# A fused attention, expert and feed-forward kernel: another order of copies, casts and sums in its last stage

## The chip, the cores and the metric

The kernel runs on one core of a Trainium2 chip. The metric is the device time of one execution in microseconds (us), the median of several runs. The engines are called as in the profile: PE is TensorE (matmuls; PEld its weight loads), ACT ScalarE, DVE VectorE, POOL GpSimd, SP the engine that issues most DMAs. SBUF is the on-chip memory, PSUM the memory that matmuls write to.

## What is computed

Three parts run one after the other: an attention over pooled keys, a layer of eight experts, and a feed-forward layer. The change lies in the last, which takes 4608 tokens of 512 values through 2048 hidden values:

```python
def _moe2_ref(x, w_in, w_out):          # x 4608x512, w_in 512x2048, w_out 2048x512
    h = x @ w_in
    g = h * (1.0 / (1.0 + np.exp(-h)))  # silu
    return (g @ w_out).astype(np.float32)
```

## The kernel before

**Numbers as pairs.** Every float32 operand of a matmul is a pair: a high part (a cast on ACT to the type fp32r) and a low part (the rest, a subtraction on DVE or POOL). A product is three matmuls into one PSUM tile: high by high, high by low, low by high. So nothing goes to PE before ACT has cast it and, two matmuls later, DVE has made its low part.

**Visits.** Tokens are taken in nine blocks of 512. The first three go through the feed-forward layer directly, in four visits (the loop over `visits` in `ffn`, line 1599; the first block in two visits, of 6 and 10 steps, the others in 16 each). One step `f` handles 128 hidden values: `mm1` (12 matmuls into a tile fh; then silu on ACT into fsg, a cast into fgh, a subtraction on DVE into fgl) and `mm2` of the step before (12 matmuls into fop), so 24 matmuls of 128x512 a step. Beside this, visits 0 and 1 build the pairs of the layer's weights (DVE, ACT, POOL) and write them to DRAM, and during the last two visits a generator `sums()` (line 1314) forms sums of the weights for what follows. One of its 16 steps adds high and low parts on DVE (two instructions into a tile sw), forms four sums on POOL, casts them on ACT and subtracts on DVE (into a tile shl), and writes the pair with two DMAs. In the kernel before, a step begins with the cast and subtraction of the sums made just before it; the tile sw has one buffer (tag fr0).

**Double blocks.** The other six token blocks are taken two by two, each pair as a 2x2 block matrix, by the seven-product scheme of Strassen and Winograd, in both matmuls of the layer. There are 12 rounds `m` (line 1657): three double blocks, with four rounds of 512 hidden values each. A round has three runs of matmuls on PE:

- `strassen(2m)`, here *even*: seven products of 6 matmuls (tiles ps), from the token sums (xc) and the weight sums (win),
- `strassen(2m+1)`, here *odd*: the same with the next weights (w1l),
- `second(m)`: seven parts of 12 matmuls (tiles fopy), 6 with the even and then 6 with the odd combination c_k of the hidden values, and the weights wout.

Between them, ACT, DVE and POOL turn products into hidden values (copies tm, silu into hs), add these into the combinations (`sum1` to `sum4`, into cs and in place) and make the pair c_0 to c_6 of each (`combo`: the cast on ACT; it returns the subtraction on DVE, called the low part; `split2`: both at once). `evict` adds a finished part of `second` into an accumulator accc, on ACT as a copy where a double block begins. Four parts of `second` add onto the PSUM tile of two parts before, so such a part begins after that eviction.

**What sets the order.** Each engine executes in the order in which the code records instructions: there is no scheduler behind it. The code is written as a sequence with hooks: `strassen` calls `hook(i)` after its i-th product and `second` calls `hook(e)` after half parts, and the work of the run before is recorded there. So an instruction that waits holds back all behind it on its engine; SP's DMAs likewise.

## Time and profile before

| what | value |
|---|---|
| median of 3 runs | 1355.88 us (1355.69 to 1356.69) |
| the profiled execution: its own time | 1355.27 us |
| its span in the trace | 1353.3 us |
| PE busy | 1238.0 us, 91% of the span |
| DVE busy | 932.7 us, 69% |
| ACT busy | 612.7 us, 45% |
| POOL busy | 390.5 us, 29% |
| mean share of the 16 DMA engines (queue q1) | 56.6% |
| mean granted PE clock | 0.967 of full |

The span runs from the first to the last instruction in the trace. Matmuls overlap, so PE counts as busy a little longer than its matmuls are apart; the granted clock is the share of 2.4 GHz that PE was given. In the trace an idle stretch stands in brackets behind the instruction that ended it, with the engine and tile that released it.

### The profile page before, as it was taken

Reading aid. Unit: us, or ns where it says so; the run is one execution under the profiler, and the core shown is the slowest. Engines: PE = TensorE matmul, PEld = TensorE weight load, DVE = VectorE, ACT = ScalarE, POOL = GpSimd, SP = SyncE. Lnnn points to the kernel's source line nnn. Section 1 sums busy time; section 2 is a strip of 40 time slices with the busy share of each in tenths; the row PEclk is TensorE's granted clock in tenths of the full one; section 3 lists DMA queues with packets and bytes.
Section 4 is the critical chain, followed back from the end, with each engine's and each line's share of the span. In section 5 each row is a group of like instructions: output and inputs, shape, how many; then the busy total and the mean of one; then the engine's idle time right before and its main releaser. Section 6 shows DMA issues by size and latency. Waiting matters only on the chain.

```text
span 1353.3 us, 20365 instructions
## 1 busy us (share of the span) xinstructions
PE 1238.0 (91%) x6165; PEld 1031.2 (76%) x6166; DVE 932.7 (69%) x1568; ACT 612.7 (45%) x1284; POOL 390.5 (29%) x349
## 2 busy tenths in 40 slices
PE   6999899999899899999779998898889888988896
PEld 6988778888888787888558787787677767766784
DVE  6888875666767597884455356577874786857557
ACT  5878433554555455444232244432544234534332
POOL 5476432132322223232443131211321112312210
PEclk9999999999999999999889999899999999989998
DMA  9988455556656336484666725765559654665445
GB/s 376 321 307 280 139 176 185 191 182 206 215 176 234 133 91 198 137 289 159 209 233 186 210 82 180 185 200 180 170 144 229 221 167 129 196 207 168 133 150 132
DMA packets 164304, 260.69 MB, mean 193 GB/s; under 512 B 43717, under 2 KB 92997, under 8 KB 161536
## 3 DMA queue, kind: packets, MB, share of 16 engines
q1 hardware_dynamic: 156928, 242.70, 56.6%
q0 software_dynamic: 7008, 16.80, 3.9%
q8 instruction: 41, 0.67, 0.2%
q14 instruction: 39, 0.32, 0.1%
q10 hardware_dynamic: 288, 0.20, 0.0%
HBM read 203.16 MB, written 59.18 MB: 194 GB/s over the span
## 4 chain that ended last, share of the span: by engine, by line
PE 33%; DVE 16%; ACT 8%; POOL 4%; issue 2%; DMA 2%; SPq 0%; DVEq 0%; ACTq 0%; POOLq 0%
PE fopy L117 14%; PE ps L117 6%; DVE c L117 6%; PE fop L117 6%; PE fh L117 5%; POOL sw L117 4%; ACT c L117 3%; DVE hs L117 1%; DVE shl L117 1%; PE yp L117 1%; DVE accc L117 1%; ACT shl L117 1%; ACT hs_a L117 1%; DVE hs_a L117 1%; DVE sw L117 1%
## 5 line engine op out<-in xcount | busy, mean ns | idle before, releaser
L117 PE MATMUL fopy<-c,wout 128*128 128x512 f32 x810 | 213.9, 419 | 39.9 <-ACT c L117 36.5
L117 PEld LDWEIGHTS fopy<-c,wout 128*128 128x128 f32 x810 | 162.5, 204 | 86.3 <-ACT c L117 40.8
L117 DVE TENSOR_TENSOR c<-hs,c 128x512 fp32r<-128x512 f32 x96 | 85.5, 890 | 50.2 <-ACT c L117 50.2
L117 POOL TENSOR_TENSOR tm<-tm,tm 128x512 f32<-128x512 f32 x24 | 31.0, 1292 | 259.3 <-ACT tm L117 259.3
L117 DVE TENSOR_TENSOR accc<-fopy,accc 128x1024 f32<-128x1024 f32 (+1 forms) x73 | 87.8, 1202 | 22.1 <-PE fopy L117 20.4
L117 ACT CAST c<-hs 128x512 fp32r<-128x512 f32 x96 | 58.7, 614 | 69.0 <-DVE hs L117 36.9
L117 DVE TENSOR_TENSOR w2l<-raw,w2h 128x512 fp32r<-128x512 f32 x96 | 65.7, 690 | 28.9 <-ACT w2h L117 26.3
L117 ACT ACTIVATE hh<-hp 128x256 fp32r<-128x256 f32 (+1 forms) x96 | 39.4, 410 | 99.3 <-PE hp L117 88.1
L117 PE MATMUL fop<-fh,fgh 128*128 128x512 f32 x168 | 69.9, 416 | 15.6 <-ACT fgh L117 15.6
L117 PE MATMUL fh<-w1l,fh 128*128 128x512 f32 x336 | 83.5, 391 | 0.0
L117 PE MATMUL yp<-w2h,hh 128*128 128x512 f32 x208 | 83.0, 399 | 0.1
L117 PE MATMUL yp<-w2l,hh 128*128 128x512 f32 x208 | 81.2, 391 | 2.0 <-DVE w2l L117 2.0
L117 ACT COPY tm<-ps 128x512 f32<-128x512 f32 x72 | 42.0, 584 | 88.6 <-PE ps L117 88.3
L117 PE MATMUL yp<-w2h,hl 128*128 128x512 f32 x208 | 81.3, 391 | 0.0
L117 PE MATMUL hp<-xth,w1h 128*128 128x256 f32 (+2 forms) x384 | 73.0, 312 | 8.5 <-PEq L1831 3.6
L117 POOL TENSOR_TENSOR sw<-sw 128x256 f32<-128x256 f32 x64 | 54.2, 866 | 78.2 <-DVE sw L117 77.0
L117 PE MATMUL hp<-xtl,w1h 128*128 128x256 f32 (+2 forms) x384 | 72.2, 309 | 3.1 <-DVE xtl L117 1.9
L117 PEld LDWEIGHTS fh<-w1l,fh 128*128 128x128 f32 x336 | 63.9, 190 | 13.6
L117 DVE TENSOR_TENSOR c<-cs,c 128x512 fp32r<-128x512 f32 x48 | 56.0, 1166 | 23.6 <-ACT c L117 23.3
L117 ACT ACTIVATE fsg<-fh 128x512 f32<-128x512 f32 x48 | 28.6, 596 | 94.0 <-PE fh L117 89.8
L117 PE MATMUL hp<-xth,w1l 128*128 128x256 f32 (+2 forms) x384 | 71.0, 307 | 0.0
L117 ACT ACTIVATE prb<-s,mx 128x72 f32<-128x72 f32 x288 | 65.2, 353 | 10.5 <-DVE mx L117 10.5
(244 smaller groups left out, 2930.9 us busy)
## 6 DMA issues: line engine op xcount, KB each, us to landing
raw<-w SPq DMA_DIRECT2D x88, 512.0 KB
wout<-wdo SPq DMA_DIRECT2D x135, 256.0 KB
win<-wdi SPq DMA_DIRECT2D x36, 512.0 KB
w1l<-wdi SPq DMA_DIRECT2D x36, 512.0 KB
xa<-x SPq DMA_DIRECT2D x36, 256.0 KB
v<-vR SPq DMA_DIRECT2D x7, 1280.0 KB
w1l<-wdo SPq DMA_DIRECT2D x33, 256.0 KB
fr<-w_in SPq DMA_DIRECT2D x16, 512.0 KB
```

Source lines behind the costliest of these rows:

```text
L117: ins = f(*a, **k)
```

## The change

Three things, in `ffn` alone.

- **Double blocks.** On ACT and DVE the copies, silus, casts, low parts and sums of a round stand in another order. The cast of c_0 follows its silu at once, in both halves of a round. Of the even half, c_6 and c_1 are cast earlier, and c_3, c_4 and c_5 ahead of the odd half's first silu; of the odd half, sum1, sum3 and the cast of c_1 are recorded within `strassen`, sum2, c_2 and c_3 one hook earlier. Some evictions move behind or ahead of a low part. PE's and POOL's orders are unchanged.
- **Weights' sums.** A step of `sums` now adds and sums first and then casts and subtracts what the step before it made. The pair is put in place of the sums, in one of three buffers (fr0 to fr2 in turn); the tile shl is gone. There is one step of the generator for each f (before, two at f = 8 and 10 of visit 2), so its 17 steps end at f = 7 of the last visit and not at f = 5. The loads of the first two double-block tokens (stx) move from f = 6 to f = 7 and 8, and the four transposes of the first from f = 8 and 9 to f = 9.
- **Tokens of the second visit.** Their load (fx_0) is issued at f = 0 of the first visit, not at f = 2.

The diff, cut to its core:

```diff
@@ -1312,27 +1312,16 @@
             def sums():
-                g, last = nc.gpsimd, None
+                g, v, last = nc.gpsimd, nc.vector, None
                 for n in range(17):
-                    if last:
-                        w, p, side = last
-                        t = self.fpool.tile([P, 2, 2 * DM], F32R, name=f"shl{n}", tag=f"fr{1 + n % 2}")
-                        sm = w[:, 2:4].rearrange("p a n -> p (a n)")
-                        nc.scalar.copy(t[:, 0], sm)
-                        nc.vector.tensor_tensor(t[:, 1], sm, t[:, 0].bitcast(F32), ALU.subtract)
...
+                    now = None
                     if n < 16:
                         p, side = divmod(n, 2)
-                        w = self.fpool.tile([P, 4, DM], F32, name=f"sw{n}", tag="fr0")
+                        w = self.fpool.tile([P, 4, DM], F32, name=f"sw{n}", tag=f"fr{(n + 1) % 3}")
...
-                        last = w, p, side
+                        now = w, p, side
+                    if last:
+                        w, p, side = last
+                        h, l = [w[:, 2 * i:2 * i + 2].rearrange("p a n -> p (a n)") for i in range(2)]
+                        nc.scalar.copy(h.bitcast(F32R), l)
+                        v.tensor_tensor(l.bitcast(F32R), l, h, ALU.subtract)
...
+                    last = now
                     yield
@@ -1485,8 +1485,8 @@
                 nc.scalar.copy(p7, pc)
+                nc.gpsimd.tensor_tensor(p7, p5, p7, ALU.add)
                 hook(2)
-                nc.gpsimd.tensor_tensor(p7, p5, p7, ALU.add)
@@ -1494,37 +1494,51 @@
                 silu(0, pa)
+                low0 = combo(n, 0)
                 hook(4)
+                low0()
                 prod(pb, s_4, "b22", False)
+                nc.vector.tensor_tensor(base("a21", "fgl"), pb, p1, ALU.add)
                 silu(6, t[6])
-                nc.vector.tensor_tensor(base("a21", "fgl"), pb, p1, ALU.add)
+                if n % 2 == 0:
+                    low6 = combo(n, 6)
                 silu("a21", t["a21"])
-                split2(n, 0)
-                hook(5)
+                if n % 2 == 0:
+                    low6()
                 prod(pc, a22, "t4", False)
+                low = None
+                if n % 2 == 0:
+                    sum1(n)
+                    low = combo(n, 1)
                 nc.vector.tensor_tensor(base(5, "fa", bufs=1), pc, p1, ALU.add)
+                if n % 2 == 0:
+                    sum3(n)
+                    return lambda: silu(5, t[5]), low
                 silu(5, t[5])
-                if n % 2 == 0:
-                    split2(n, 6)
-
-            def pair(n):
+                sum1(n)
+                sum3(n)
+                return combo(n, 1)
+
+            def pair(n, first):
 
                 def hook(i):
                     if i == 0:
-                        sum1(n)
-                        sum3(n)
-                        split2(n, 1)
+                        first[0]()
+                        first[1]()
+                        sum2(n)
                     if i == 1:
-                        sum2(n)
                         low = combo(n, 2)
                         sum4(n)
                         low()
                     if i == 2:
-                        split2(n, 3)
+                        rest.extend(combo(n, j) for j in (3, 4))
                     if i == 3:
-                        split2(n, 4)
+                        rest.pop(0)()
+                        rest.pop(0)()
+                        rest.append(combo(n, 5))
                     if i == 4:
-                        split2(n, 5)
+                        rest.pop(0)()
@@ -1602,13 +1616,13 @@
-                        for _ in range(0 if f == fs[-1] and v == 2 else 2 if v == 2 and f in (8, 10) else 1):
+                        for _ in range(0 if f == fs[-1] and v == 2 else 1):
                             next(adds, None)
-                    if f == fs[0] + 2:
+                    if f == (fs[0] + 2 if v else 0):
                         load_x(after if after is not None else doubles[0][0])
@@ -1621,14 +1635,16 @@
-                        if f == 6:
-                            load_stage(0, 0)
-                            load_stage(0, 1)
+                        if f in (7, 8):
+                            load_stage(0, f - 7)
...
-                        if 8 <= f < 12:
+                        if f == 9:
+                            for k in range(4):
+                                stage_x(0, 0, k)
+                        if f in (10, 11):
                             for k in range(2):
-                                stage_x(0, f // 2 - 4, 2 * (f % 2) + k)
+                                stage_x(0, 1, 2 * (f % 2) + k)
@@ -1674,36 +1690,38 @@
                 def hook1(e, ps):
                     k = e // 2
                     if e == 0:
-                        sum1(n)
-                        sum3(n)
-                        split2(n, 1)
+                        low1()
+                        sum2(n)
                     if e == 1:
-                        sum2(n)
+                        lows.append(combo(n, 2))
                     if e % 2 and k < 6:
                         evict(ps, PARTS[k][1], q == 0)
                     if e == 1:
-                        low = combo(n, 2)
                         sum4(n)
-                        low()
-                    if e == 2:
-                        split2(n, 3)
+                        lows.pop()()
+                        lows.append(combo(n, 3))
+                    if e == 3:
+                        lows.pop()()
+                        lows.append(combo(n, 4))
                     if e == 4:
-                        split2(n, 4)
+                        lows.pop()()
```

How it moves instructions, at three places. ACT around the odd half's start of round m = 1 (the odd half's silus are hs_0_6391, hs_6_6380 and hs_a_6403 before, hs_0_6377, hs_6_6365 and hs_a_6389 now; c_3 to c_5 are the even half's). Before:

```order
L117 COPY tm_2_6336<-ps_2_6332 128x512
L117 CAST c_3_6369<-cs_1_6344 128x512
L117 CAST c_4_6382<-hs_a_6304 128x512
L117 ACTIVATE hs_0_6391<-ps_0_6330 128x512
L117 CAST c_5_6393<-hs_5_6316 128x512
L117 ACTIVATE hs_6_6380<-hs_6_6380 128x512
L117 ACTIVATE hs_a_6403<-hs_a_6403 128x512
L117 CAST c_0_6406<-hs_0_6391 128x512
L117 ACTIVATE hs_5_6415<-hs_5_6415 128x512
L117 CAST c_1_6429<-cs_1_6426 128x512
```

And now:

```order
L117 COPY tm_2_6324<-ps_2_6320 128x512
L117 CAST c_3_6354<-cs_1_6303 128x512
L117 CAST c_4_6356<-hs_a_6290 128x512
L117 CAST c_5_6369<-hs_5_6307 128x512
L117 ACTIVATE hs_0_6377<-ps_0_6318 128x512
L117 CAST c_0_6379<-hs_0_6377 128x512
L117 ACTIVATE hs_6_6365<-hs_6_6365 128x512
L117 ACTIVATE hs_a_6389<-hs_a_6389 128x512
L117 ACTIVATE hs_5_6399<-hs_5_6399 128x512
L117 CAST c_1_6405<-cs_1_6402 128x512
```

The cast of the odd c_0 stood behind the silus of hs_6 and hs_a (a21 in the code); it now stands ahead of both. DVE at the same place, before:

```order
L117 TENSOR_TENSOR c_3_6369<-cs_1_6344,c_3_6369 128x512
L117 TENSOR_TENSOR tm_0_6334<-ps_3_6333,tm_0_6334 128x512
L117 TENSOR_TENSOR c_4_6382<-hs_a_6304,c_4_6382 128x512
L117 TENSOR_TENSOR c_5_6393<-hs_5_6316,c_5_6393 128x512
L117 TENSOR_TENSOR hs_a_6403<-ps_1_6331,tm_0_6334 128x512
L117 TENSOR_TENSOR c_0_6406<-hs_0_6391,c_0_6406 128x512
L117 TENSOR_TENSOR hs_5_6415<-ps_2_6332,tm_0_6334 128x512
```

And now:

```order
L117 TENSOR_TENSOR tm_0_6322<-ps_3_6321,tm_0_6322 128x512
L117 TENSOR_TENSOR c_3_6354<-cs_1_6303,c_3_6354 128x512
L117 TENSOR_TENSOR c_4_6356<-hs_a_6290,c_4_6356 128x512
L117 TENSOR_TENSOR c_5_6369<-hs_5_6307,c_5_6369 128x512
L117 TENSOR_TENSOR c_0_6379<-hs_0_6377,c_0_6379 128x512
L117 TENSOR_TENSOR hs_a_6389<-ps_1_6319,tm_0_6322 128x512
L117 TENSOR_TENSOR hs_5_6399<-ps_2_6320,tm_0_6322 128x512
```

The odd c_0's low part goes ahead of the odd hs_a, and tm_0, which POOL needs, ahead of c_3. DVE during the weights' sums, f = 3 to 5 of the last visit, before:

```order
L117 TENSOR_TENSOR fgl_3_5423<-fsg_3_5420,fgh_3_5422 128x512
L117 TENSOR_TENSOR shl_5426<-sw_5383,shl_5426 128x1024
L117 TENSOR_TENSOR sw_5431<-fh_4607,fl_4608 128x512
L117 TENSOR_TENSOR sw_5431<-fh_4651,fl_4652 128x512
L117 TENSOR_TENSOR fgl_4_5466<-fsg_4_5463,fgh_4_5465 128x512
```

And now:

```order
L117 TENSOR_TENSOR fgl_3_5388<-fsg_3_5385,fgh_3_5387 128x512
L117 TENSOR_TENSOR sw_5391<-fh_4479,fl_4480 128x512
L117 TENSOR_TENSOR sw_5391<-fh_4525,fl_4526 128x512
L117 TENSOR_TENSOR sw_5344<-sw_5344 128x1024
L117 TENSOR_TENSOR fgl_4_5430<-fsg_4_5427,fgh_4_5429 128x512
```

The additions into the new sw come first, and the subtraction behind them belongs to the tile of the step before (5344, not 5391).

## Rows read from the trace of the kernel before

**Rows 1.** Stretches m = 2, m = 5, all twelve: engines' busy us, PEclk, DMA share, GB/s.

```profile
892.91:937.25 44.34, 40.68 (x169) 32.37 (x169) 34.57 (x41) 15.96 (x28) 8.02 (x6) 0.96 0.50 168
...
1029.91:1074.26 44.35, 40.69 (x169) 32.36 (x169) 29.06 (x36) 16.96 (x29) 8.02 (x6) 0.96 0.90 240
...
sum 543.75, PE 493.63 PEld 391.18 DVE 370.40 ACT 217.19 POOL 107.59; mean PE 41.14 PEld 32.60 DVE 30.87 ACT 18.10 POOL 8.97
```

**Rows 2.** Chain of work that ended last, round m = 2: start us, us, what.

```profile
892.91 8.17 PE ps L117 x36
...
909.42 0.62 ACT c L117
...
915.38 0.61 DVE hs_a L117
...
916.07 0.63 ACT hs_a L117
916.70 0.52 ACT c L117
...
917.26 19.99 PE fopy L117 x78
```

**Rows 3.** Waits, 802 to 1345 us: engine, tile, releaser: total us, times, longest.

```profile
PE fopy L117 <- ACT c L117: 43.9, 12, 3.7
```

**Rows 4.** Timeline of POOL and DVE in round m = 2.

```profile
897.75 1.29 POOL L117 TENSOR_TENSOR tm<-tm,tm 128x512 f32<-128x512 f32 x1 [22.03 <-ACT tm L117]
...
906.94 1.30 POOL L117 TENSOR_TENSOR hs_a<-hs,hs_a 128x512 f32<-128x512 f32 x1 [6.36 <-DVE cs L117]
...
898.45 0.69 DVE L117 TENSOR_TENSOR tm<-ps,tm 128x512 f32<-128x512 f32 x1 [2.48 <-PE ps L117]
...
907.48 1.30 DVE L117 TENSOR_TENSOR c<-cs,c 128x512 fp32r<-128x512 f32 x1 [0.69 <-ACT c L117]
...
921.63 1.21 DVE L117 TENSOR_TENSOR accc<-fopy,accc 128x1024 f32<-128x1024 f32 x1
```

**Rows 5.** Busy time by stretch (columns as rows 1): visits 1, 2 and 3.

```profile
535.03:631.60 96.57, 94.38 (x409) 77.69 (x408) 74.97 (x74) 44.37 (x62) 26.86 (x10) 0.98 0.68 215
631.60:713.51 81.91, 64.35 (x242) 49.88 (x240) 42.19 (x56) 25.42 (x38) 36.94 (x44) 0.84 0.58 196
713.51:757.83 44.32, 42.40 (x181) 33.55 (x180) 22.10 (x29) 15.33 (x22) 17.26 (x20) 1.00 0.59 189
757.83:801.49 43.66, 43.66 (x194) 36.19 (x193) 22.29 (x24) 16.41 (x23) 8.40 (x3) 1.00 0.52 127
```

**Rows 6.** Timeline of PE in visit 2: start, us, instruction [idle before <-releaser].

```profile
657.25 0.79 PE L117 MATMUL fop<-fh,fgh 128*128 128x512 f32 x1 [3.73 <-ACT fgh L117]
657.84 0.63 PE L117 MATMUL fop<-fl,fgh 128*128 128x512 f32 x1
658.27 0.63 PE L117 MATMUL fop<-fh,fgh 128*128 128x512 f32 x1
```

**Rows 7.** Timelines of DVE, POOL and ACT in visit 2: one step of the sums.

```profile
683.48 1.22 DVE L117 TENSOR_TENSOR shl<-sw,shl 128x1024 fp32r<-128x1024 f32 x1 [3.89 <-ACT shl L117]
684.74 1.29 DVE L117 TENSOR_TENSOR sw<-fh,fl 128x512 f32<-128x512 f32 x2
685.96 1.23 DVE L117 TENSOR_TENSOR fgl<-fsg,fgh 128x512 fp32r<-128x512 f32 x1
690.40 1.22 DVE L117 TENSOR_TENSOR shl<-sw,shl 128x1024 fp32r<-128x1024 f32 x1 [3.22 <-ACT shl L117]
...
685.58 3.70 POOL L117 TENSOR_TENSOR sw<-sw 128x256 f32<-128x256 f32 x4 [3.21 <-DVE sw L117]
...
689.32 1.05 ACT L117 CAST shl<-sw 128x1024 fp32r<-128x1024 f32 x1 [4.71 <-POOL sw L117]
```

**Rows 8.** Timelines of SP and DVE at the end of visit 0.

```profile
526.41 2.52 SPq L117 DMA_DIRECT2D fx<-xa  x4
...
536.66 1.30 DVE L117 STREAM_TRANSPOSE xt<-fx 128x512 f32<-128x512 f32 x2 [5.09 <-DMA fx<-xa]
```

More of the change, by code (lines that the diff above doesn't have):

```diff
@@ L1314, in sums @@
             def sums():
-                g, last = nc.gpsimd, None
+                g, v, last = nc.gpsimd, nc.vector, None
                 for n in range(17):
-                    if last:
-                        w, p, side = last
-                        t = self.fpool.tile([P, 2, 2 * DM], F32R, name=f"shl{n}", tag=f"fr{1 + n % 2}")
-                        sm = w[:, 2:4].rearrange("p a n -> p (a n)")
-                        nc.scalar.copy(t[:, 0], sm)
-                        nc.vector.tensor_tensor(t[:, 1], sm, t[:, 0].bitcast(F32), ALU.subtract)
-                        for l in range(2):
-                            if side:
-                                nc.sync.dma_start(self.wdo[p, :, 0:4, l],
-                                                  t[:, l].bitcast(F32).rearrange("p (c n) -> p c n", n=256))
-                            else:
-                                nc.sync.dma_start(self.wdi[p, :, 2 + l], t[:, l].bitcast(F32))
+                    now = None
                     if n < 16:
                         p, side = divmod(n, 2)
-                        w = self.fpool.tile([P, 4, DM], F32, name=f"sw{n}", tag="fr0")
+                        w = self.fpool.tile([P, 4, DM], F32, name=f"sw{n}", tag=f"fr{(n + 1) % 3}")
                         sm = w[:, 2:4].rearrange("p a (c n) -> p (a c) n", n=256)
@@ L1334, in sums @@
                             h, l = self.fw[2 * p + j]
-                            nc.vector.tensor_tensor(w[:, j], h[:, side].bitcast(F32), l[:, side].bitcast(F32), ALU.add)
+                            v.tensor_tensor(w[:, j], h[:, side].bitcast(F32), l[:, side].bitcast(F32), ALU.add)
                         a11, a12, a21, a22 = [w[:, j, 256 * k:256 * (k + 1)] for j in range(2) for k in range(2)]
@@ L1346, in sums @@
                             g.tensor_tensor(sm[:, 3], a12, sm[:, 1], ALU.subtract)
-                        last = w, p, side
+                        now = w, p, side
[4 more added lines that the diff above has]
+                        v.tensor_tensor(l.bitcast(F32R), l, h, ALU.subtract)
+                        for i, t in enumerate((h, l)):
+                            if side:
+                                nc.sync.dma_start(self.wdo[p, :, 0:4, i], t.rearrange("p (c n) -> p c n", n=256))
+                            else:
+                                nc.sync.dma_start(self.wdi[p, :, 2 + i], t)
+                    last = now
                     yield
@@ L1522, in hook @@
                     if i == 2:
-                        split2(n, 3)
+                        rest.extend(combo(n, j) for j in (3, 4))
                     if i == 3:
-                        split2(n, 4)
+                        rest.pop(0)()
+                        rest.pop(0)()
+                        rest.append(combo(n, 5))
                     if i == 4:
-                        split2(n, 5)
+                        rest.pop(0)()
+                rest = []
                 return hook
@@ L1646, in ffn @@
                     load_out(4)
-                    strassen(0)
+                    first = strassen(0)
                     load_in(2)
@@ L1676, in hook0 @@
                         some(jobs[0])
-                    if i == 5 and q == 0 and d:
+                    if i == 4 and q == 0 and d:
                         write("c12", old, d - 1)
@@ L1683, in ffn @@
                         load_stage(d + 1, 1)
-                    strassen(2 * m, hook0)
+                    first = strassen(2 * m, hook0)
                     load_in(2 * m + 2)
-                strassen(2 * m + 1, pair(2 * m))
+                low1 = strassen(2 * m + 1, pair(2 * m, first))
                 n = 2 * m + 1
+                lows = []
                 def hook1(e, ps):
```

## The prediction, made before the changed kernel was run

> **What bounds the kernel now.** I read the busy shares first: PE is busy for 91% of the span and the other engines for at most 69%, so what can be won is PE's idle time, and I looked for the stretches that hold it. The table of stretches shows two. Each of the twelve rounds of the double blocks takes 44.34 us or a little more [rows 1]. PE's own pace stands in the chain of waits: 36 matmuls in 8.17 us, 0.227 us each [rows 2]. A round has 168 matmuls (42 even, 42 odd, 84 in `second`), 38.1 us at that pace; so a plain round loses 6.2 us, and all twelve lose 543.75 - 12 x 38.1 - 2.7 (12 matmuls of the last visit's end stand in the first) = 83.8 us. In visits 2 and 3, where the weights' sums run, 420 matmuls (10 and 7.5 steps of 24) take 81.91 + 44.32 us [rows 5] against 95.3: 30.9 lost. Visit 1's 408 matmuls take 96.57 [rows 5] against 92.6: 4.0 lost. The last stretch of visit 3 loses nothing: 43.66 us, PE busy in all of it [rows 5].
>
> Where the round's loss sits is read from the chain and the waits. Both name one place: PE waits 3.7 us in each of the twelve rounds for ACT's cast of a combination c [rows 3]. In the chain it is the odd c_0: DVE makes hs_a, ACT silus it, and only then casts c_0, after which `second` goes on at 917.26 [rows 2]. Hs_a isn't needed for c_0; it merely stands ahead of it on ACT. And hs_a itself was late because DVE was still at the even half's low parts. After such a pause PE also runs slowly: behind a wait of 3.73 us in visit 2 its matmuls were 0.43 us apart (657.84, 658.27) [rows 6], the lower of its two levels, 1.2 in place of 2.4 GHz. The rest of the loss is this slow stretch and parts of `second` that wait for an eviction: the 78 matmuls after the pause take 19.99 us [rows 2], 2.3 over their pace.
>
> **The rounds, step by step.** I count from the round's start, 0 = 892.91. PE, if it never waits, ends the even products at 1.36, 2.72 ... 9.53 (the fifth, from which c_0 comes, at 6.81), the odd ones up to 19.05 (third 13.61, fourth 14.97, fifth 16.33), and needs the odd c_0 at 20.41, after six matmuls with the even one, and its low part 0.45 later. Durations: a cast 0.62, a silu 0.63 [rows 2], a DVE instruction of 128x512 0.69, or 0.61 behind another [rows 2, 4], one on POOL 1.3 [rows 4].
>
> One thing governs the middle of it: a low part of DVE took 1.30 us beside a POOL instruction that began at 906.94, nearly twice the 0.69, while DVE's tm at 898.45, with one input in PSUM, took 0.69 within POOL's 897.75 to 899.04 [rows 4]. So instructions with two SBUF inputs wait for POOL, the others don't. I count each such wait below.
>
> The Trainium skill has this as a rule (GPSIMD Engine Reference, "8. Key points"): GpSimd shares its SBUF interfaces with VectorE, and they contend where a VectorE instruction has two SBUF inputs. By that rule the trace agrees, in both rows; and it speaks against this change, which brings low parts closer to POOL's work.
>
> Even half, in the new order: silu 7.4, cast of c_0 8.1, its low part 8.8; hs_a 9.4, silu 10.0, sum1 10.7, cast of c_1 11.4; its low part waits for POOL's sum3 (10.9 to 12.2), 12.75; sum2 13.3, sum4 13.95. ACT then casts c_3, c_4, c_5 by 16.0, before the odd fifth product ends at 16.33: so silu at 17.0 and the odd c_0's cast at 17.6, 2.8 us before it is needed. DVE: tm at 15.7, then three low parts, held up by POOL's two additions (14.6 to about 17.7), end near 19.0, the odd c_0's low part at 19.7, needed at 20.86. **The pause goes**, and with it PE's slow stretch. The hs_5 of the even half, which now stands behind sum1, is done at 11.3; PE wants its PSUM tile again at 12.25.
>
> What is late next: odd hs_a 20.2, silu 20.9, sum1 21.6, cast of c_1 22.2 (wanted 23.1), its low part behind POOL's sum3 at 23.6 (wanted 23.6), sum2 24.2, first eviction 1.21 us [rows 4], 25.3; the third part wants its PSUM tile at 24.5. So PE still waits 0.8 us a round there; for hand-overs I take 1.0. That should be too short to slow PE: the stretch from 713.51 to 757.83 lost 3.5 us to short waits and was granted 1.00 [rows 5].
>
> Not touched: rounds with other work in them. The sum is 9 us above twelve plain rounds and those 12 matmuls (543.75 - 532.1 - 2.7) [rows 1]; this I keep. I add 1 us for the three rounds whose first eviction is a copy on ACT behind c_2, and 2 us for round 5, whose DMA engines are busy 0.90 of its 44.35 us [rows 1] and have 39 us for the same bytes afterwards. What remains of 83.8 is 12 + 9 + 3 = 24; **gain 59 to 60 us**.
>
> **The weights' sums.** Before, the step is one chain, since the sums have one buffer: additions on DVE 1.29, four sums on POOL 3.70, cast 1.05, subtraction 1.22, and again [rows 7]: from subtraction to subtraction 690.40 - 683.48 = 6.9 us, while PE needs 24 x 0.227 = 5.44 for a step. The next step's fgh and fgl queue behind it. Now cast and subtraction belong to the step before, so POOL has done their input, and three buffers let additions go ahead. Per step DVE has 1.2 + 1.2 + 0.6 (fgl) = 3.0 us and POOL 3.70 less the fgl that held it up (1.23 in place of 0.69) [rows 7], 3.1. If they overlap at all beyond 0.7 us, 5.44 is held; even at 5.7 the lag of some 2.5 us over nine steps fits before PE misses fgl: that is made 1.9 us after its product (silu, cast, low part) and wanted 4.5 after it, behind 20 matmuls. Buffers: the writes of step n must have landed before n + 3 adds, two PE steps later, some 8 us; the 4 DMAs that load tokens in between (fx took some 8 us to land, 528.9 to 536.7 [rows 8]) may cost one wait. The stx loads go out a step or two later, the first two steps (10.9 us) ahead of its use; fx took 10 us from issue to DVE's start [rows 8], and the 2.6 us that fgl has in hand cover some lateness. I keep 3 us of the 30.9 for the change of visits and these; **gain 28**.
>
> **The second visit's tokens.** DVE waited 5.09 us for fx, which SP had issued at 526.41, behind weight loads that wait for a buffer [rows 8]. At f = 0 it goes out some 10 us earlier and lands before the transposes' turn. On SP it passes one pair of weight loads, which wait for their buffer anyway. The bounds are nothing, if the tokens were written only by then, and 4.0 us; near the upper one, since DVE's wait is the only one of that stretch on PE's path, I take **3.8**.
>
> **The sum.** 1355.3 (the profiled execution's own time, 0.6 below the median) - 59.4 - 28 - 3.8 = 1264.1; I forecast 1264.
>
> **Rivals.**
> - *The wait moves down the chain* (chance 0.18). DVE's low parts lose to POOL each time: odd c_0's low part at 20.8, c_1's at 24.8, the first eviction at 26.6, two us of PE a round over what I took: 1264 + 12 x 2 = 1288. For it: the 1.30 at 907.48 [rows 4]. Against: POOL is busy 8 of 44 us only [rows 1].
> - *DVE and POOL take turns in the sums* (0.15). If no instruction of one overlaps the other, a step is 3.1 + 3.0 = 6.1 us, not 5.44: 17 steps x 0.66 = 11 us, and slow matmuls after pauses some 4: 1279. Against: these durations hold start-up time, which may overlap. By the rule of the Trainium skill (GPSIMD Engine Reference, "8. Key points") at its strictest it would come out this way.
> - *Slower: PE loses its clock* (0.03). With no pauses PE could be granted less than its full level for long. From 535 us on PE has 92.6 + 95.3 + 43.7 + 460 = 692 us of matmuls; the change gives back 91 us, so it decides below a mean granted clock of 692 / 783 = 0.88 there; at 0.85 the price is 692 / 0.85 - 692 = 122 us, and the time 1386. Against: at 757.83 to 801.49 PE was busy throughout and granted 1.00 [rows 5].
> - *It doesn't do it* (0.02): the odd c_0's cast now stands behind those of c_3 to c_5, and c_3's waits for sum4; if sum4 came 6 us later than I count, PE would pause as before, and the rest of the change would be given back by late evictions: about 1355.
>
> **How the numbers follow.** My forecast has 0.62, with 1250 to 1277 as its own range: it ends where nothing of the rounds' waits remains (12 us) and half of what I kept in the sums, and where a round keeps 2 us. The second and third case reach 1288 and 1279, both at once 1303. A range of 1250 to 1300 leaves out the last two rivals, half of the two at once, and gains larger than I see. A measurement of this kernel tells 0.2%, 2.7 us, from no change. Faster by more: 0.95; within: 0.02; slower: 0.03.
>
> **What would show it.** Right: no wait of PE for c in the table of waits (43.9 us now), rounds of 39 to 40 us at a granted clock of 0.99 or 1.00, visits 2 and 3 up to f = 8 in 96 to 99 us, no DVE wait for fx. Wrong: a PE wait of over 2 us in most rounds, whoever releases it; DVE's low parts at 1.3 us throughout; visit 2 at over 60 us; or granted clock below 0.95 where PE has no pause.

## The result, and the profile after

The changed kernel takes **1257.33 us** (median of 4 runs, 1253.46 to 1260.40), the kernel before beside it 1355.79 us (median of 4): a ratio of **0.9275**, 95% interval 0.9245 to 0.9305, faster. The profiled execution took 1256.2 us (its span is 1254.4), 99.1 us less than the one of the kernel before. The forecast was 1264, 7 us or 0.5% above the median.

The page's busy shares and the granted clock (tenths in 40 slices) of the changed kernel:

```profile
PE 1199.6 (96%) x6165; PEld 1013.7 (81%) x6166; DVE 937.2 (75%) x1568; ACT 616.7 (49%) x1284; POOL 413.0 (33%) x349
...
PEclk9999999999999999999999999999999999999999
```

DVE and ACT are busy as long as before, in 99 us less; POOL is busy 22 us longer, and we come to why. The mean granted clock rose from 0.967 to 0.994.

Busy time by stretch of the changed kernel (columns as in rows 1): visits 1, 2 and 3 (this in two pieces), the rounds m = 2 and m = 5, and all twelve.

```profile
535.79:628.27 92.48, 92.48 (x410) 76.60 (x409) 70.99 (x68) 44.26 (x62) 26.75 (x10) 1.00 0.67 214
628.27:683.32 55.05, 54.73 (x242) 44.98 (x241) 42.95 (x45) 23.56 (x36) 39.92 (x36) 1.00 0.76 253
683.32:724.12 40.80, 40.80 (x181) 33.79 (x181) 35.05 (x39) 16.63 (x23) 31.53 (x28) 1.00 0.68 219
724.12:767.64 43.52, 43.52 (x194) 36.05 (x193) 23.97 (x26) 17.46 (x24) 9.40 (x4) 1.00 0.59 164
850.76:889.72 38.96, 38.42 (x169) 31.38 (x169) 33.69 (x41) 16.27 (x28) 8.09 (x6) 1.00 0.57 190
969.98:1009.94 39.96, 38.71 (x169) 31.30 (x169) 28.28 (x36) 17.28 (x29) 8.09 (x6) 1.00 0.97 268
767.64:1246.36 478.72, 467.07 (x2029) 377.81 (x2027) 359.23 (x443) 220.24 (x366) 110.61 (x77) 1.00 0.65 199
```

Against [rows 1, 5], the gains are 543.75 - 478.72 = 65.0 us in the rounds, 81.91 + 44.32 - 55.05 - 40.80 = 30.4 in visits 2 and 3, and 96.57 - 92.48 = 4.1 in visit 1: 99.5 in sum, the whole difference of the two executions within half a microsecond. A plain round takes 38.96 us, 0.9 above PE's own pace of 38.1. In the visits PE is busy throughout, but for 0.3 us.

What PE still waits for in the rounds is small. Its waits from 760 to 1250 us in the changed kernel (engine, tile, releaser: total us, times, longest):

```profile
PE fopy L117 <- DVE accc L117: 4.9, 9, 0.5
PE fopy L117 <- ACT accc L117: 2.9, 3, 1.0
PE fopy L117 <- DVE c L117: 1.6, 4, 0.6
PE fopy L117 <- DMA wout<-wdo: 1.4, 2, 0.7
PE fopy L117 <- DMA w1l<-wdo: 0.9, 1, 0.9
```

The row of [rows 3], 43.9 us for ACT's cast, is gone. The chain in round m = 2 of the changed kernel shows what is last now (start us, us, what):

```profile
850.76 14.97 PE ps L117 x66
...
872.14 0.63 ACT c L117
...
872.80 1.23 DVE c L117
874.03 0.60 DVE hs L117
874.63 1.15 DVE accc L117
...
875.83 13.90 PE fopy L117 x60
```

PE does all its products without a pause, and waits once, 0.54 us, for the first eviction (accc). It is late because c_1's low part takes 1.23 us. The timeline rows of POOL and DVE there:

```profile
872.19 1.30 POOL L117 TENSOR_TENSOR hs_a<-hs,hs_a 128x512 f32<-128x512 f32 x1 [3.82 <-DVE cs L117]
...
872.80 1.23 DVE L117 TENSOR_TENSOR c<-cs,c 128x512 fp32r<-128x512 f32 x1 [0.69 <-ACT c L117]
873.96 0.68 DVE L117 TENSOR_TENSOR hs<-cs,hs 128x512 f32<-128x512 f32 x1
874.56 1.21 DVE L117 TENSOR_TENSOR accc<-fopy,accc 128x1024 f32<-128x1024 f32 x1
```

### The profile page after: what moved, and what is told of

It is laid out like the page before. It is cut to its first block, busy times and chain, and to the rows that moved or that the text cites. A ratio compares the mean times of both kernels' runs of the same rounds, so it can differ in the third digit from the quotient of the medians.

```text
span 1254.4 us, 20320 instructions
## 1 busy us (share of the span) xinstructions
PE 1199.6 (96%) x6165; PEld 1013.7 (81%) x6166; DVE 937.2 (75%) x1568; ACT 616.7 (49%) x1284; POOL 413.0 (33%) x349
## 4 chain that ended last, share of the span: by engine, by line
PE 42%; DVE 12%; DMA 3%; ACT 2%; issue 2%; POOL 1%; SPq 0%; DVEq 0%; POOLq 0%; ACTq 0%
PE ps L117 12%; PE fopy L117 10%; PE fh L117 8%; PE fop L117 8%; DVE c L117 5%; DVE accc L117 2%; PE hp L117 1%; DMA wout<-wdo 1%; PE yp L117 1%; DVE cs L117 1%; ACT c L117 1%; DVE sw L117 1%; POOL sw L117 1%; DVE tm L117 1%; DVE hs L117 1%
## 5 line engine op out<-in xcount | busy, mean ns | idle before, releaser
L117 PE MATMUL fopy<-c,wout 128*128 128x512 f32 x810 | 194.6, 392 | 8.4 <-DVE accc L117 3.8
L117 PEld LDWEIGHTS fopy<-c,wout 128*128 128x128 f32 x810 | 150.2, 188 | 47.0 <-DVE accc L117 6.8
L117 ACT ACTIVATE hh<-hp 128x256 fp32r<-128x256 f32 (+1 forms) x96 | 39.4, 411 | 100.1 <-PE hp L117 89.1
L117 DVE TENSOR_TENSOR c<-hs,c 128x512 fp32r<-128x512 f32 x96 | 67.9, 717 | 25.0 <-ACT c L117 25.0
L117 POOL TENSOR_TENSOR sw<-sw 128x256 f32<-128x256 f32 x64 | 72.4, 1156 | 35.9 <-DVE sw L117 34.6
L117 DVE TENSOR_TENSOR fgl<-fsg,fgh 128x512 fp32r<-128x512 f32 x48 | 39.3, 818 | 41.4 <-ACT fgh L117 41.4
L117 PEld LDWEIGHTS hp<-xth,w1h 128*128 128x128 f32 x384 | 60.9, 193 | 10.4 <-issue 8.8
```

The costliest lines, as they stand in the source:

```text
L117: ins = f(*a, **k)
```

## The experiments

Three questions. Are the three gains independent, and each of the size that the traces give? Is it c_0's place alone that paid, in the rounds, and the delay or the buffers, in the sums? And what holds the last half microsecond of a round? In the table, *visits* is the time from the first matmul of visit 0 to the first of round 0, and *round* that of m = 2 from its first matmul to the next round's, both from PE's timeline of the profiled execution; the ratio is to the kernel before in the same session (whose median was 1351.7, 1353.1 and 1353.4 us in the three).

| kernel | median us | ratio, 95% interval | visits us | round us |
|---|---|---|---|---|
| before | 1355.79 | 1 | 293.5 | 44.35 |
| changed | 1257.33 | 0.9275, 0.9245 to 0.9305 | 259.1 | 38.96 |
| e1_rounds | 1287.43 | 0.9521, 0.9484 to 0.9557 | 293.3 | 39.02 |
| e2_sums | 1318.21 | 0.9759, 0.9720 to 0.9797 | 260.3 | 44.35 |
| e3_fx | 1348.98 | 0.9973, 0.9953 to 0.9992 | 289.0 | 44.34 |
| e4_c0 | 1331.30 | 0.9847, 0.9809 to 0.9885 | 293.7 | 43.12 |
| a0_change (changed, again) | 1254.86 | 0.9272, 0.9247 to 0.9298 | 258.5 | 38.97 |
| e5_late | 1269.35 | 0.9378, 0.9355 to 0.9400 | 259.0 | 40.23 |
| e7_same | 1285.50 | 0.9500, 0.9482 to 0.9518 | 290.1 | 39.00 |
| e8_evict | 1252.57 | 0.9256, 0.9238 to 0.9274 | 258.8 | 38.76 |
| e9_sum3 | 1252.45 | 0.9252, 0.9232 to 0.9272 | 258.5 | 38.42 |
| e11_both | 1253.70 | 0.9253, 0.9230 to 0.9275 | 258.4 | 38.43 |
| e6_two | 1267.94 | 0.9372, 0.9348 to 0.9396 | 271.2 | 38.96 |
| e10_dve | 1254.37 | 0.9280, 0.9257 to 0.9304 | 260.6 | 38.99 |

**The three parts alone.** Each puts one part of the change into the kernel before. e1_rounds: all that the diff does in `strassen`, `pair`, `hook0` and `hook1`.

> The kernel before with the rounds' new order alone (strassen, pair, hook0, hook1); sums and the token load stay as before. Theory (three independent gains, which the two traces put at 65.0 us in the rounds, 30.4 in visits 2 and 3, 4.1 in visit 1): 1355.8 - 65.0 = 1291, rounds of 39.0 us. Rival (they depend on each other: the rounds' stretch gained because the weight loads that follow the sums came earlier): rounds of 40 us and more, 1300 or above.

e2_sums: all that it does in `sums`, and the loads and transposes of the double blocks' first tokens.

> The kernel before with the sums' change alone (three buffers, cast and subtraction a step later, the double blocks' tokens loaded at f = 7 and 8). Theory: 1355.8 - 30.4 = 1325.4, visits 2 and 3 up to f = 8 in 96 us against 126, rounds unchanged at 543.8 in sum. Rival (the sums' wait hid other waits, which take its place, or the first rounds lose what the visits win): 1335 or above.

e3_fx is this line:

```diff
-                    if f == fs[0] + 2:
+                    if f == (fs[0] + 2 if v else 0):
                         load_x(after if after is not None else doubles[0][0])
```

> The kernel before with the second visit's tokens loaded at f = 0 in place of f = 2, alone. Theory: DVE's wait of 5.09 us for fx goes and visit 1 takes 92.5 us in place of 96.6: 1355.8 - 4.1 = 1351.7. Rival (part of the 4.1 us comes from the sums' change, or the tokens are late anyway): 1353.5 to 1356.

Measured, as gains of the ratio times 1355.8: 64.9, 32.7 and 3.7 us, 101.3 in sum; the whole change has 98.3 (94.2 to 102.4). Within their intervals the gains add up. The traces say it more sharply than the medians, which also hold the up to 7 us by which the start of the kernel differs from run to run (the first matmul of visit 0 came between 501 and 508.5 us): e1's visits are those of before and its round that of the changed kernel, e2's round is that of before, and e3 takes 4.5 us off the visits. In e3 DVE went to the transposes of fx without a wait, where it had waited 5.09 us [rows 8]. e3's own median is the one number that a single part leaves loose, 1.1 to 6.4 us.

One number needs care. e2's visits, 260.3 us, are only 1.2 us above those of the changed kernel, though e2 loads fx as late as the kernel before. In its execution that load cost less. DVE waited 4.06 us for it in place of 5.09, and PE after it 1.15 us (DVE, then PE):

```profile
531.03 1.30 DVE L117 STREAM_TRANSPOSE xt<-fx 128x512 f32<-128x512 f32 x2 [4.06 <-DMA fx<-xa]
...
533.56 1.20 PE L117 MATMUL fop<-fh,fgl 128*128 128x512 f32 x4 [1.15 <-DVE fgl L117]
```

In the kernel before, PE waited 2.19 us at this place:

```profile
539.20 1.59 PE L117 MATMUL fop<-fh,fgl 128*128 128x512 f32 x4 [2.19 <-DVE fgl L117]
```

The step that leads from visit 0 into visit 1 took 8.2 us without the wait, 10.0 in e2, and 12.2, 12.4 and 12.5 in the kernel before, e1 and e4. So the late load costs 1.9 us in one execution and 4.1 to 4.3 in three. From that step on, e2 gains 31.0 us and the changed kernel 30.4: there the sums' gain is the same.

**One move of the rounds alone.** In the kernel before, the odd c_0 goes behind its silu:

```diff
                 silu(0, pa)
+                if n % 2:
+                    split2(n, 0)
                 hook(4)
...
-                split2(n, 0)
+                if n % 2 == 0:
+                    split2(n, 0)
                 hook(5)
```

> The kernel before with one move: in the odd halves the cast of c_0 and its low part stand right behind c_0's silu, ahead of the even c_5, all else as before. Theory A (c_0's place was the whole of the wait): PE's waits of 3.7 us for c go, with their slow stretch, and the gain is 50 to 65 us: 1291 to 1306. Theory B (the wait moves down the chain, since hs_a, sum1 and c_1 on DVE and ACT are as late as before: c_1 is then wanted at about 2.7 us behind c_0's turn and comes some 2 us late): PE waits 2 us a round for c_1, and the gain is 12 x 1.5 to 12 x 3 = 18 to 36 us: 1320 to 1338.

The gain is 1.53%, 20.7 us, and the round falls by 1.2 us of the 5.4: theory B. The wait moved down the chain, as PE's timeline of e4_c0 in round m = 2 shows (start, us, instruction, idle before):

```profile
907.54 1.20 PE L117 MATMUL fopy<-c,w1l 128*128 128x512 f32 x4 [1.40 <-DVE c L117]
908.57 1.52 PE L117 MATMUL fopy<-c,wout 128*128 128x512 f32 x6
910.78 0.73 PE L117 MATMUL fopy<-c,wout 128*128 128x512 f32 x2 [0.69 <-ACT c L117]
912.04 1.20 PE L117 MATMUL fopy<-c,wout 128*128 128x512 f32 x4 [0.52 <-DVE c L117]
913.77 3.06 PE L117 MATMUL fopy<-c,wout 128*128 128x512 f32 x12 [0.54 <-DVE accc L117]
```

One wait of 3.66 became four of 3.15 in sum: for c_0's low part, c_1's cast, c_1's low part, and the eviction. The longest of the four is for c_0's own low part, which theory B did not name. Together they are 0.5 us shorter than the one; the rest of the 1.2 is the slow stretch, for this round was granted 1.00 and the same round of the kernel before 0.96 [rows 1]. DVE's rows say why: it makes the low parts of c_0 and c_5 beside POOL (2.36 us for the two, where 1.3 would do), and only then hs_a, from which c_1 comes.

```profile
905.73 2.36 DVE L117 TENSOR_TENSOR c<-hs,c 128x512 fp32r<-128x512 f32 x2
908.01 0.68 DVE L117 TENSOR_TENSOR hs_a<-ps,tm 128x512 f32<-128x512 f32 x1
```

In e4 hs_a begins 23.17 us into the round (908.01 - 884.84), in the changed kernel 19.44 (870.04 - 850.60). So the move of c_0 needs the rest of the order with it, by which the even half's work is out of DVE's way earlier.

**The same move undone.** In the changed kernel, the odd c_0 goes back behind the silus of hs_6 and hs_a:

```diff
-                low0 = combo(n, 0)
+                if n % 2 == 0:
+                    low0 = combo(n, 0)
                 hook(4)
-                low0()
+                if n % 2 == 0:
+                    low0()
...
                 if n % 2 == 0:
                     low6()
+                else:
+                    split2(n, 0)
```

> The changed kernel with one thing put back: in the odd halves c_0's cast and low part again behind the silus of hs_6 and hs_a; all else as changed. By the first trace hs_a's silu ends at 20.8 us of a round (871.38 - 850.60), so the cast would come at 21.4 and the low part at 22.0, where PE wants them at 20.4 and 20.9. Theory (both are needed, the place of c_0 and the shorter work ahead of hs_a): a wait of about 1 us for the cast and a few tenths for the low part in each round, c_1 and the evictions 0.6 us or more behind that: 12 x 1.5 = 18 us, plus or minus 8, above the changed kernel; no wait of 3.7. Rival (the place alone decides): the 3.7 us waits come back with their slow stretch, 50 to 65 us above the changed kernel.

1.06% of 1353 is 14.3 us; the round is 40.23 us, 1.27 more. That is inside the theory's 10 to 26, and the rival's 50 to 65 is out. (The waits that the trace lists came smaller than expected, 0.25 us for the cast and 0.16 for a low part of c_1 in round m = 2. By the starts of its matmuls, PE loses 0.4 us ahead of c_0, 0.4 within c_0's six matmuls and 0.3 at c_1's low part, 1.1 of the 1.27; the eviction costs what it did, a wait of 0.54.) So of the 65 us, c_0's place is worth some 14 us where all else is in its new order and 21 where nothing else is; the larger share, 44 us or more, comes from the rest of the new order. Which of its other moves brings how much was not tried one by one.

**The sums: the delay.** Three buffers kept, but a step casts and subtracts what it has just summed:

```diff
-                        now = w, p, side
-                    if last:
-                        w, p, side = last
                         h, l = [w[:, 2 * i:2 * i + 2].rearrange("p a n -> p (a n)") for i in range(2)]
...
-                    last = now
```

> The changed kernel with the sums' cast and subtraction in the same step as the sums, three buffers kept. Theory (the delay by a step is what takes the chain off PE's path): the step is additions, four sums, cast, subtraction in one chain again, some 6.9 us where PE needs 5.44, and visits 2 and 3 lose about 25 to 31 us: 25 us or more above the changed kernel. Rival (the single buffer was the limit): with three buffers the next step's additions go ahead, and the time is that of the changed kernel within 5 us.

2.28% is 31 us, and the visits take 290.1 us where the kernel before would have 289.4 without its wait for fx (293.5 - 4.1): **all of the sums' gain is gone, three buffers or not**. DVE's subtractions of e7_same in visit 2, each behind ACT's cast, come every 7.0 to 7.2 us:

```profile
649.26 1.23 DVE L117 TENSOR_TENSOR sw<-sw 128x1024 fp32r<-128x1024 f32 x1 [4.14 <-ACT sw L117]
...
656.22 1.23 DVE L117 TENSOR_TENSOR sw<-sw 128x1024 fp32r<-128x1024 f32 x1 [3.92 <-ACT sw L117]
...
663.46 1.22 DVE L117 TENSOR_TENSOR sw<-sw 128x1024 fp32r<-128x1024 f32 x1 [4.19 <-ACT sw L117]
```

While DVE stands in such a wait, the next step's additions and fgl stand behind it, free buffer or not.

**The sums: the buffers.** The delay kept, two buffers in turn:

```diff
-                        w = self.fpool.tile([P, 4, DM], F32, name=f"sw{n}", tag=f"fr{(n + 1) % 3}")
+                        w = self.fpool.tile([P, 4, DM], F32, name=f"sw{n}", tag=f"fr{1 + n % 2}")
```

> The changed kernel with two buffers for the sums in place of three, the delay by a step kept. A step's write goes out about 7.5 us after its additions and needs some 4 us to land by an estimate from the waits of the changed kernel's trace (DVE waited 2.12 us for one with three buffers beside token loads); with two buffers the next use comes 10.9 us after. Theory (delay and buffers both count): DVE waits for writes in most steps, and visits 2 and 3 lose 5 to 20 us. Rival (the delay alone decides): within 2 us of the changed kernel. Second rival (two buffers undo the whole gain): 25 us or more above it.

1.00%, 13.5 us, and the visits 12.2 us longer: the first theory. DVE's waits of e6_two from 620 to 765 us:

```profile
DVE sw L117 <- DMA wdi<-sw: 17.7, 7, 5.7
DVE sw L117 <- DMA wdo<-sw: 14.4, 6, 4.4
```

In the changed kernel the same view has one such wait, of 2.1 us. So the delay brings the gain, and the third buffer keeps 12 us of it.

**The sums: POOL's part on DVE.** One word in the changed kernel:

```diff
-                g, v, last = nc.gpsimd, nc.vector, None
+                g, v, last = nc.vector, nc.vector, None
```

> The changed kernel with the weights' four sums of a step on DVE in place of POOL. In the changed kernel a sum on POOL took 1.07 us (median; 0.74 before) and an addition on DVE 1.22 (0.69 before). Theory (that growth is the two engines holding each other up): with DVE alone the addition is back at 0.69, the cast's input is ready earlier, DVE's step is about 1.3 + 4 x 0.4 + 1.2 + 0.7 = 4.8 us, under PE's 5.44, and the time stays within 3 us of the changed kernel. Rival (DVE has no room for 1.6 us more a step): visits 2 and 3 take 5 to 15 us more.

The ratio is that of the changed kernel within its interval, the visits are 1.5 us longer. The sums' instructions by shape, in nanoseconds (lowest, median, highest), of the changed kernel

```profile
L117 POOL TENSOR_TENSOR sw<-sw x64: 729/1070/1729, 634.4 to 724.0; 128x256 f32<-128x256 f32 x64
L117 DVE TENSOR_TENSOR sw<-fh,fl x28: 678/1220/1226, 632.9 to 719.1; 128x512 f32<-128x512 f32 x28
```

and of e10_dve, where POOL has nothing to do there (the median of the first row is that of the 128x256 sums, which are 64 of its 80):

```profile
L117 DVE TENSOR_TENSOR sw<-sw x80: 415/422/1226, 627.1 to 718.0; 128x256 f32<-128x256 f32 x64, 128x1024 fp32r<-128x1024 f32 x16
L117 DVE TENSOR_TENSOR sw<-fh,fl x28: 679/685/691, 625.7 to 712.9; 128x512 f32<-128x512 f32 x28
```

With POOL out of it, every addition takes 0.68 to 0.69 us; beside POOL most take 1.22, and POOL's sums 1.07 in place of the 0.74 of the kernel before, where the two engines took turns because the chain made them. That makes 17 of POOL's 22 us more (39.92 + 31.53 against 36.94 + 17.26 in visits 2 and 3 [rows 5]). It costs PE nothing within the steps, whose 5.44 us have room for both ways; e10's 1.5 us stand where visit 2 changes to 3, where PE waited 1.9 us for DVE's fgl.

**The last half microsecond.** First by order: the first eviction ahead of sum2.

```diff
                     if e == 0:
                         low1()
-                        sum2(n)
...
                     if e == 1:
+                        sum2(n)
+                        lows.append(combo(n, 2))
                         sum4(n)
```

(The cast of c_2, `lows.append(combo(n, 2))`, leaves its place ahead of the eviction.)

> The changed kernel with the first eviction of second (accc of part 0) ahead of sum2 on DVE in hook1, in place of behind it. The change left a PE wait of 0.54 us in each plain round for that eviction, whose instruction began 0.60 us behind sum2 (873.96, 874.56). Theory: that wait goes, and c_2, which is then 1.2 us later, still comes in time: 9 rounds x 0.5 = 4 to 5 us below the changed kernel. Rival (the wait moves on to c_2's cast or its low part, or to the second eviction): the same time within 1.5 us, or up to 6 us more.

0.9256 against 0.9272, where 4 to 5 us less were expected: not told apart. The wait for the eviction goes, but a plain round falls by 0.2 us only, since smaller waits come behind it. And rounds m = 3 and m = 7 take 40.6 us in place of 38.96, though this order was meant to help them as well. There the new position meets POOL. Timeline rows of e8_evict in round m = 3 (POOL, DVE, then PE):

```profile
914.88 2.40 POOL L117 TENSOR_TENSOR xct<-st,xct 128x1024 fp32r<-128x1024 f32 x1 [6.76 <-ACT xct L117]
...
915.16 3.20 DVE L117 TENSOR_TENSOR xcb<-st,xcb 128x1024 fp32r<-128x1024 f32 x1
...
920.15 3.03 PE L117 MATMUL fopy<-c,wout 128*128 128x512 f32 x12 [1.45 <-DVE accc L117]
```

and of the changed kernel at the same place, where DVE is there first, by 0.17 us (DVE, POOL):

```profile
919.32 1.21 DVE L117 TENSOR_TENSOR xcb<-st,xcb 128x1024 fp32r<-128x1024 f32 x1
920.46 0.68 DVE L117 TENSOR_TENSOR c<-hs,c 128x512 fp32r<-128x512 f32 x1
...
919.49 3.92 POOL L117 TENSOR_TENSOR xct<-st,xct 128x1024 fp32r<-128x1024 f32 x1 [7.04 <-ACT xct L117]
```

The same two instructions: the one that starts second takes longer. DVE's xcb takes 1.99 us more, where 2.12 of POOL's were left; POOL's xct takes 1.52 more, where 1.65 were left of xcb and of the low part that follows it on DVE. When the second is DVE's, the eviction behind it is 2 us late and PE waits 1.45.

Then by the contention itself: the odd sum3 on POOL is made to start behind sum2, worked out from other operands.

```diff
-                nc.gpsimd.tensor_tensor(t[4], t[0], t["a21"], ALU.subtract)
+                a, b = (t[6], t[2]) if n % 2 else (t[0], t["a21"])
+                nc.gpsimd.tensor_tensor(t[4], a, b, ALU.subtract)
...
                 sum1(n)
-                sum3(n)
                 return combo(n, 1)
...
                         low1()
                         sum2(n)
+                        sum3(n)
```

> The changed kernel with POOL's subtraction sum3 of the odd halves moved from the moment of c_1's low part to behind sum2: it is worked out as hs_6 less the new hs_0 (the same value, since c_1's sum is hs_a plus hs_6), so POOL can begin only when DVE has made sum2, and runs beside the eviction, which reads PSUM. Theory (POOL's instruction beside c_1's low part is what costs PE the last 0.54 us of a plain round: 1.23 us in place of 0.68): the low part takes 0.7, the eviction begins 0.55 us earlier, the wait goes, and a plain round falls from 38.97 to 38.2 to 38.5: 5 to 8 us below the changed kernel. Rival (the wait is DVE's own order, or POOL now delays sum4 and c_2's low part as much): the same within 2 us.

DVE and POOL of e9_sum3 in round m = 2:

```profile
867.36 0.69 DVE L117 TENSOR_TENSOR c<-cs,c 128x512 fp32r<-128x512 f32 x1 [0.69 <-ACT c L117]
...
869.70 0.93 DVE L117 TENSOR_TENSOR cs<-hs,hs 128x512 f32<-128x512 f32 x1
...
868.79 1.29 POOL L117 TENSOR_TENSOR hs_a<-hs,hs 128x512 f32<-128x512 f32 x1 [5.87 <-DVE hs L117]
```

The cause is shown: without POOL beside it c_1's low part takes 0.69 us, and the round falls to 38.42, by the 0.54 that PE had waited. The time, though, is 0.9252, where 5 to 8 us less were expected: again not told apart from 0.9272. Rounds 3 and 7 meet the same clash as in e8 (40.3 us each; DVE's xcb 3.41 us), and in round m = 5, whose DMA engines are busy 0.90 of the time, PE waited 3.79 us for weights in this execution:

```profile
994.88 8.20 PE L117 MATMUL fopy<-c,wout 128*128 128x512 f32 x24 [3.79 <-DMA wout<-wdo]
```

Round 5 took 45.0 us here, 42.7 in e11_both and in e7_same, 40.0 and 40.6 in the two executions of the changed kernel and 39.4 in e8_evict; whether the order or the execution makes that difference isn't shown. What the plain rounds give, some 0.5 us each, these rounds take back.

e11_both adds to this the first eviction ahead of c_2's cast in the rounds with q = 0, where it is a copy on ACT.

```diff
-                    if e == 1:
+                    if e == 1 and q:
                         lows.append(combo(n, 2))
                     if e % 2 and k < 6:
                         evict(ps, PARTS[k][1], q == 0)
+                    if e == 1 and not q:
+                        lows.append(combo(n, 2))
```

> As the run before it, and besides in the three rounds with q = 0 the first eviction, a copy on ACT, ahead of c_2's cast. There PE waited 0.97 us each for that copy. Theory: those waits go too, 2 to 3 us more: 7 to 11 us below the changed kernel. Rival (c_2's cast is then late in those rounds, and PE waits for it instead): as the run before it.

0.9253, where 2 to 3 us less than e9 were expected: nothing beyond e9 that this can tell. Its waits for ACT's accc are 3.3 us in four, against 3.9 in five in e9_sum3: the one of round 0 is gone, those of rounds 4 and 8 are as long as they were (1.6 and 1.7 us in two waits each, where e9 has 1.5 and 1.5). So no version here is surely better than the changed kernel; three lie 0.2% below it, with intervals that overlap its own.

## Why the prediction was right

**What bounds the kernel.** Right: the idle of PE was all there was to win, in the two places named, and it was won there. DVE's and ACT's busy times changed by less than 5 us.

**The rounds: 65.0 us where 59.4 was forecast.** The mechanism is the one given, an order on ACT and DVE and not a lack of either, and the counted times held: odd hs_a was put at 20.2 us of the round and its end is at 20.1 (870.04 + 0.68 - 850.60); c_1's low part was put beside POOL's sum3, to end at 23.6, and ends at 23.4. So the remaining wait was at the place named, the third part's for the first eviction, and 0.54 us in place of 0.8. One reading of the kernel before was too wide: the 2.3 us behind the pause were put down to the slow stretch and to waits for evictions, and in round m = 2 the trace has no wait longer than 0.15 us there, but a granted clock of 0.81. Two sizes were off. Hand-overs, 12 x 1.0: a plain round keeps 38.97 - 38.1 = 0.87, 10.4 in all. And the 9 us for other work and the 3 beside it, 12: measured 478.72 - 12 x 38.97 - 2.7 = 8.4. What was kept as one lump was not one. Rounds 3 and 7 had 1.6 us each over a plain one before and have none now, round 8 fell from 3.1 to 2.6, and round 4 kept its 2.3; round 0, which had none, now has 2.5, with waits for DVE's c and for ACT's copy; round 5 has 1.0, 0.7 of it a wait for a DMA, where I had put 2 for its DMAs; the waits for copies on ACT, put at 1 us more, rose from 1.1 us to 2.9. So of the 9 us that were kept some 4 went, which was not foreseen, and nearly 4 came where 3 were put. (The last 0.4 of the 5.6 us is rounding: 83.8 - 24 is 59.8, and the sum took 59.4.)

**The sums: 30.4 where 28 was forecast.** Right, with the cause stated half wrong. The text blamed the one buffer for the chain; e7_same shows that with three buffers the chain is the same, 7.0 us a step, as long as cast and subtraction stand behind their own sums on DVE. The buffers only let the delay work, and e6_two sizes that. Of the 3 us kept, 0.65 came (8.81 us between two steps where visit 2 changes to 3, in place of 8.16). The one wait for a buffer beside the token load was there: DVE, 2.12 us, and PE didn't notice.

**The tokens: 4.1 where 3.8 was forecast.** Right for these two executions; the trace of e3_fx gives 4.5 for the visits, its median 3.7 with a wide interval. But the size hangs on when the load lands: in e2_sums the same late load cost 1.9 us.

**The rivals.** *The wait moves down the chain* came true in e4_c0, where c_0's move stands alone, and in no round of the change itself: there hs_a follows early enough. *DVE and POOL take turns*: they contend more than I allowed (additions at 1.22, sums at 1.07 us), yet no step of PE in visits 2 and 3 is longer than 5.44 but the one between the two visits. In visit 2, DVE was busy for 43.0 and POOL for 39.9 of 55.05 us, waits for each other included. The Trainium skill (GPSIMD Engine Reference, "8. Key points") says that GpSimd and VectorE contend where a VectorE instruction has two SBUF inputs. The trace agrees (an addition takes 1.22 us beside POOL and 0.69 in e10_dve without it), but that this makes a step longer, the rival's point, it doesn't bear out. *PE loses its clock*: at 96% busy it was granted 0.994, more than before. *It doesn't do it*: sum4 came in time.

**The signs.** No wait for fx and a clock of 1.00: as named. PE's waits for ACT's cast of c are gone, but not every wait for c, as the sign had it: 1.6 us for DVE's low parts are left, in four waits, two of them in round 0. Rounds at 38.97 us and visits 2 and 3 up to f = 8 at 95.85 lie just under the bands of 39 to 40 and 96 to 99. Each of the three terms that were kept was taken a little too large, all on one side: 5.2 us in the rounds, 2.4 in the sums, 0.3 for the tokens.

## What to carry to other kernels

An engine that executes in recorded order makes everything behind a waiting instruction late: look for the cast or copy whose input has long been there and that stands behind one whose input is late, but count the whole chain before you move it, since the one move alone gave a third of what the reorder gave. Where two engines hand a tile back and forth within a step, take the second half of the step one step later; more buffers without that delay gave nothing here, and the delay with too few buffers gave 60% of it. When an order is within a fraction of a microsecond of a clash between DVE and POOL, an edit that helps in one round can lose it again in another, so read all rounds and not the plain one alone.

## What the runs showed of the hardware

**DVE and POOL wait for whole instructions of each other, where DVE's has two SBUF inputs.** In the two sets of rows above (e8_evict and the changed kernel), xcb on DVE takes 1.21 us if it starts first and 3.20 if it starts 0.28 behind POOL's 2.40; xct on POOL takes 2.40 us if first and 3.92 if second. In the second case DVE's next instruction, the low part at 920.46, went ahead of the waiting POOL as well, and took its 0.68. In e9_sum3, sum4 begins at 869.70 beside POOL's 868.79 to 870.08 and takes 0.93: the 0.38 until POOL's end, and 0.55. The evictions, which read PSUM, take their 1.21 us beside POOL as well.

**A long pause of PE cost more than its own length, a short one did not.** After the wait of 3.79 us in e9_sum3 the next 24 matmuls took 8.04 us where 5.44 is their pace; in visit 2 of e7_same PE paused for 1.2 to 1.5 us in step after step, and its matmuls went on 0.23 us apart. The stretches, columns as in rows 1: e9_sum3 behind that wait,

```profile
994.88:1002.92 8.04, 8.04 (x24) 6.40 (x25) 3.57 (x5) 1.24 (x2) 0.00 (x0) 0.67 0.60 188
```

and three steps of e7_same, with their pauses:

```profile
650.42:671.50 21.08, 17.29 (x72) 13.28 (x72) 9.05 (x13) 6.46 (x9) 9.25 (x12) 1.00 0.98 296
```

The granted clock was 0.67 behind the long pause, so PE ran a good part of that stretch at the lower of its two levels, 1.2 in place of 2.4 GHz, and 1.00 beside the short ones. Two stretches of the kernel before, behind the pause of 2.19 us for fx and behind the 3.66 us of round m = 2:

```profile
539.20:544.56 5.36, 5.36 (x16) 4.25 (x17) 4.83 (x8) 1.61 (x3) 0.00 (x0) 0.68 0.34 125
917.26:926.09 8.83, 8.83 (x30) 6.62 (x31) 7.98 (x11) 2.92 (x5) 1.27 (x1) 0.81 0.41 130
```

And one of e10_dve, behind its pause of 1.89 us:

```profile
675.12:680.56 5.44, 5.44 (x24) 4.51 (x25) 5.00 (x12) 0.14 (x2) 0.00 (x0) 1.00 0.41 147
```

So the pauses of 1.2 to 1.9 us listed here were followed by the full clock, and those of 2.19, 3.66 and 3.79 us by a lower one, each in the one execution that was traced. A round of the kernel before lost some 2 us more than its pause, and the changed kernel, whose waits in the rounds are of 1.0 us at most, was granted 1.00 in all twelve.
